# First head's query rows: SBUF-to-SBUF copies from the cast tiles instead of a read back from scratch

## The chip, the cores and the metric

One NeuronCore of one Trainium2 chip runs the whole program. The metric is the device time of one execution in microseconds. Three runs of the kernel before gave 1349.76, 1350.19 (the median) and 1351.14 us.

## The reference, cut to what matters

A gate mixes an attention branch and a SwiGLU branch over the same 2048 rows of x (512 wide). The attention has 32 query heads of 16 columns and one shared key and value head.

```
g = sigmoid((x * gate_w).sum(-1))
q = x @ wq            # 32 heads of 16
k = x @ wk;  v = x @ wv
a = softmax(q k^T / 4) v, heads joined, @ wo
b = (silu(x @ w_gate) * (x @ w_up)) @ w_down
out = g * a + (1 - g) * b
```

## The kernel before, in words

**Precision.** Products are made in float32r from a rounded part and a rest: `hi` and `lo`. A product of two such pairs is three matmuls. A head's query therefore occupies several groups of 16 rows: the rounded part, the rest, the rounded part again, and a row group of absolute values scaled by `kmax` (a bound on the keys, used in place of a row maximum). That makes 64 rows for a head, and two such sets of 64 rows (one for each pair of 512-column chunks) fill the 128 partitions of the tile `qs` (L667 multiplies `qs` with the keys `ks`).

**Making the queries.** `query(m, c)` makes the product for eight heads (m = 0 to 3) and one chunk of 512 rows of x (c = 0 to 3): 12 matmuls into a PSUM bank `pf`, of which there are three. When the last one is done, `keep` casts the bank into SBUF tiles `hh` (rounded), `hl` (rest) and a third one with the absolute values. For m = 0 the third one comes from the same buffers as `hh` and `hl`; each of these two names has seven buffers. In these tiles the partition is 8 times the row of a head plus the head, so one head's 16 rows stand 8 partitions apart. `store` then issues four DMAs of 256 KB on SyncE's queue, which write the tiles into the scratch tensor `q_d` in DRAM, sorted by head. When all chunks are there, one DMA of 512 KB reads a head's 128 rows back into `qs`: for head 0 at L643, for later heads in `load_head` (L653).

**The order at the start.** In a stage whose order is written out by hand, x is transposed, keys and values are made, then the four products of m = 0 run (called m0c0 to m0c3 here), then head 0 is loaded, and `fill(GAP)` runs three more products, m1c0 to m1c2, whole. After them the attention begins. A block of it takes two units (a unit is one head and 128 keys): scores into `pss` (two buffers, two matmuls of 64 rows each per half unit), exponentials on ScalarE (L675), and `mix`, which multiplies with the values (L687, 16 matmuls per block). The remaining products run between the scores as half matmuls of 64 rows ("low" and "high" half of the contraction). The first block has only low halves beside its scores, since a product's high half starts a fixed number of steps behind its low half. A one-element memset of `sign` on VectorE (L417) marks the end of a low half; the high half waits for it.

**What sets the order.** Each engine runs its own instructions in program order. The DMAs of SyncE's queue are issued in program order too, and an issue that waits holds up those behind it. The loads of the feed-forward weights stand outside the stage written by hand, so a scheduler places them.

Of the kernel before, what the change touches and what calls it, by code (L numbers as in the profile page):

```python
# [8 lines left out]
F32 = mybir.dt.float32  # L9
# [13 lines left out]
DH = 16  # L23
# [4 lines left out]
NCH = S // CH  # L28
TC = CH // P
NF = F // P  # L30
HG = P // DH
KR = 3 * DH
RT = 64
# [29 lines left out]
def tile_gated_mix(ctx, tc, x, wq, wk, wv, wo, w_gate, w_up, w_down, gate_w, out):  # L63
    nc = tc.nc
# [9 lines left out]
    q_d = dpool.tile([H, P, 2, CH], F32, name="q_d")  # L74
# [36 lines left out]
    def three(a, b, sa, sb):  # L111
        return [(a[0][sa], b[0][sb]), (a[0][sa], b[1][sb]), (a[1][sa], b[0][sb])]

    def mm(ps, terms):
        n = len(terms)
        for i, (a, b) in enumerate(terms):
            nc.tensor.matmul(ps, a, b, start=(i == 0), stop=(i == n - 1))  # L117
# [7 lines left out]
    def run(queue, n):  # L125
        for _ in range(min(n, len(queue))):
            queue.pop(0)()
# [7 lines left out]
    def load_split(view, name, bufs, pool=wp, order=lambda w, heads=True: w):  # L135
        shape = list(view.shape)
        raw = wp.tile(shape, F32, name="wraw", bufs=WRB)
        nc.sync.dma_start(raw, view)
        hi = pool.tile(shape, F32R, name=name + "h", bufs=bufs)
        lo = pool.tile(shape, F32R, name=name + "l", bufs=bufs)  # L140
        split(order(hi, False), order(lo, False), order(raw), nc.gpsimd, nc.gpsimd)
        return hi, lo
# [63 lines left out]
            for f in self.after:  # L206
                f()

    WQ, QS = {}, {}

    def by_row(w, heads=True):
        if heads:
# [3 lines left out]
    def load_wq(m):  # L216
        WQ[m] = load_split(wq_v[:, :, m * P:(m + 1) * P], f"wq{m}", 1, qpool, by_row)

    def query(m, c):
        cs = slice(c * CH, (c + 1) * CH)  # L220
        t = m * NCH + c

        def terms():
            r = []
            for k in range(KD):
                r += three(WQ[m], XC[c], (slice(None), k), (slice(None), k))
            return r

        def keep(ps):
            qh = wp.tile([P, CH], F32R, name="hh", bufs=7)  # L230
            ql = wp.tile([P, CH], F32R, name="hl", bufs=7)

            if m:
                qb = wp.tile([P, CH], F32, name="ht" if c % 2 else "hs", bufs=2)
                nc.vector.tensor_copy(qh, ps)
            else:
                qb = wp.tile([P, CH], F32R, name="hl" if c % 2 else "hh", bufs=7).bitcast(F32)
                nc.scalar.activation(qh, ps, AF.Copy)
                nc.scalar.activation(qb.bitcast(F32R), ps, AF.Abs, scale=kmax)
            nc.vector.tensor_tensor(ql, ps, qh.bitcast(F32), ALU.subtract)  # L240
            if m:
                nc.vector.tensor_scalar(qb, qh.bitcast(F32), kmax, None, op0=ALU.mult)
                nc.vector.scalar_tensor_tensor(qb.bitcast(F32R), qb, -1.0, qb, op0=ALU.mult, op1=ALU.max)
            parts = [ql, qh, qb.bitcast(F32R)]
            def store():
                for i, j in enumerate((1, 0, 1, 2)):
                    row = c % 2 * RT + i * DH
                    nc.sync.dma_start(q_d[m * HG:(m + 1) * HG, row:row + DH, c // 2, :].rearrange("h r s -> r h s"),
                                      parts[j].bitcast(F32))

            store()
            nc.vector.tensor_reduce(top[:, t:t + 1], qb, axis=AX.X, op=ALU.max)

        return Job(3 * KD, lambda: m in WQ, terms, keep)

    def queries():
# [238 lines left out]
    def new_qs(h):  # L495
        QS[h] = qsp.tile([P, 2, CH], F32R, name="qs")
        return QS[h]

    with tc.tile_pool(name="apool", bufs=1) as ap, tc.tile_pool(name="apool2", bufs=2) as a2:
        XT = {}  # L500

        def load_x(c, n):
            XT[c] = a2.tile([P, TC, D], F32, name="xt", bufs=2)
            for i in range(0, TC, n):
                t = c * TC + i
                nc.sync.dma_start(XT[c][:, i:i + n, :], x[t * P:(t + n) * P, :].rearrange("(i p) d -> p i d", p=P))
# [12 lines left out]
        def prepare_kv():  # L519
            k, v, g = slice(0, DH), slice(DH, 2 * DH), slice(2 * DH, 2 * DH + 1)  # L520
            for r in (0, RT):
                to = [w[:, :, r:r + 3 * DH].rearrange("p k (i n) -> p k i n", i=3) for w in (wkv_h, wkv_l)]
                src = wkv_f[:, :, k].unsqueeze(2).to_broadcast([P, KD, 3, DH])
                split(to[0], to[1], src, nc.vector)
            for to, src in ((3 * DH, v), (KW - 1, g)):
                rows = slice(to, to + src.stop - src.start)
                split(wkv_h[:, :, rows], wkv_l[:, :, rows], wkv_f[:, :, src], nc.vector)
# [12 lines left out]
        def zeros(n):  # L540
            for i in range(n):
                nc.tensor.matmul(pw[:, :P], warm, warm, start=True, stop=True)

        def transpose_x(c, i):
            if i == 0:
                if c < 2:
                    new_x(c)
                else:
                    new_x(c, qpool, str(c))
            xt, (xh, xl) = XT[c], XC[c]  # L550
            pt = ps_s.tile([P, 2 * CH], F32, name="pss")
            ptv = pt.rearrange("p (k t) -> p k t", k=KD)
            for j in range(2):
                for k in range(KD):
                    nc.tensor.transpose(ptv[:, k, j * P:(j + 1) * P], xt[:, i + j, k * P:(k + 1) * P], ident)
                if c == 0:
                    zeros(KEEP)
            hi = xh[:, :, i * P:(i + 2) * P]
            nc.scalar.activation(hi, ptv, AF.Copy)
            nc.vector.tensor_tensor(xl[:, :, i * P:(i + 2) * P], ptv, hi.bitcast(F32), ALU.subtract)  # L560
# [5 lines left out]
        def project_kv(c):  # L566
            cs = slice(c * CH, (c + 1) * CH)
            if c % 2 == 0:
                VZ[c // 2] = ap.tile([KW, 2 * CH], F32, name="vz", bufs=2)
            pk = ps_f.tile([P, CH], F32, name="pf")  # L570

            terms = [(w[:, k], XC[c][0][:, k]) for k in range(KD) for w in (wkv_h, wkv_l)]
            mm(pk[:KW, :], terms + [(wkv_h[:, k], XC[c][1][:, k]) for k in range(KD)])
            vz = VZ[c // 2][:, c % 2 * CH:(c % 2 + 1) * CH]
            nc.scalar.activation(vz, pk[:KW, :], AF.Copy)
            ka = a2.tile([DH, CH], F32, name="ka")
            nc.scalar.activation(ka, pk[:DH, :], AF.Abs)
            nc.vector.tensor_reduce(nk[:, c:c + 1], ka, axis=AX.X, op=ALU.max)

            for r in (0, RT):  # L580
                nc.gpsimd.tensor_copy(ks[r:r + 3 * DH, cs], vz[r:r + 3 * DH, :])
                lo = slice(r + 2 * DH, r + 3 * DH)
                nc.gpsimd.tensor_tensor(ks[lo, cs], vz[lo, :], ks[lo, cs].bitcast(F32), ALU.subtract)
# [19 lines left out]
        with tc.manual_schedule():  # L603

            warm = ap.tile([P, P], BF16, name="warm")
            nc.vector.memset(warm, 0.0)
            pw = ps_o.tile([P, CH], F32, name="po")
            zeros(WARM)
            load_wq(0)
            transpose_x(0, 0)  # L610
            prepare_kv()
            transpose_x(0, 2)
            prepare_norms()
            load_x(2, 2)
            transpose_x(1, 0)
            transpose_x(1, 2)
            load_x(3, 2)
            project_kv(0)
            transpose_x(2, 0)
            transpose_x(2, 2)  # L620
            project_kv(1)
            transpose_x(3, 0)
            transpose_x(3, 2)
            project_kv(2)
            store_x(2)
            transpose_v(0)
            project_kv(3)
            store_x(3)
            load_wq(1)
            load_wq(2)  # L630
            for c in range(NCH):
                job = query(0, c)
                for i in range(job.size):
                    if c == 0 and i == job.size - 1:
                        spread_k()
                    job.step(i)
                if c == 0:
                    transpose_v(1)

                    nc.vector.tensor_scalar(g_sb, g_sb, 0.5, 0.5, op0=ALU.mult, op1=ALU.add)  # L640
                    nc.vector.tensor_scalar(c_sb, g_sb, -0.5, 0.5, op0=ALU.mult, op1=ALU.add)
            load_wq(3)
            nc.sync.dma_start(new_qs(0).bitcast(F32), q_d[0])  # L643
            fill(GAP)


# [2 lines left out]
    with tc.tile_pool(name="bpool", bufs=2) as bp:  # L649
# [128 lines left out]
        with tc.manual_schedule():  # L778
# [25 lines left out]
            for k in range(2 * BEGIN // BLOCK, NB):  # L804
# [8 lines left out]
                h = u // NT  # L813
# [49 lines left out]
    with tc.If(rv != 0):  # L863
        with tc.tile_pool(name="gpool", bufs=2) as gp:
            with tc.For_i(0, H, 1) as h:
# [4 lines left out]
                for qt in range(NT):  # L870
# [3 lines left out]
                    for half in range(2):  # L874
                        ps = ps_s.tile([P, 2 * CH], F32, name="pss")
                        for j in range(2):
                            c = half * 2 + j
# [60 lines left out]
```

## Time and profile before

| what | value |
|---|---|
| median of three runs | 1350.19 us |
| the profiled execution's own time | 1349.22 us |
| its span (first to last instruction) | 1347.4 us |
| TensorE busy | 1330.7 us, 99% |
| ScalarE busy | 1069.5 us, 79% |
| VectorE busy | 710.9 us, 53% |
| GpSimd busy | 223.7 us, 17% |
| mean granted TensorE clock | 0.994 of full |

The profile counts the time of each engine's instructions inside one execution. "PE" is TensorE's matmul stream, "PEld" its weight loads, "DVE" VectorE, "ACT" ScalarE, "POOL" GpSimd, "SPq" the issuing of DMAs by SyncE. A list of waits names who stood idle and whose result ended the idle time. A table by windows gives each engine's busy time in a stretch, the granted clock (1.00 is full speed) and the share of time in which the DMA engines were busy. Spans of one line are start, duration and instruction, in microseconds from the span's start.

### The profile page before, as it was taken

What the parts mean: (1) busy time and instruction counts of PE and PEld (TensorE: products, weight loads), DVE (VectorE), ACT (ScalarE), POOL (GpSimd) and SP (SyncE); (2) the same over time, 40 slices, a digit from 0 to 9 for tenths busy, and PEclk for the clock granted to TensorE, in tenths of its full rate; (3) what the DMA queues carried; (4) which work ended last, traced back from release to release, by engine and by line L of the source; (5) the groups of instructions that cost most, each with busy time, mean ns of one, the idle gap of its engine ahead of it and who ended that gap; (6) DMA issues with size and microseconds to landing.
All of it is one profiled execution on the core that took longest, in us unless ns stands there. A gap on an engine that the chain in (4) does not pass through costs nothing. (4 is left out here: it accounts for less than half of the span.)

```text
span 1347.4 us, 26625 instructions
## 1 busy us (share of the span) xinstructions
PE 1330.7 (99%) x10743; PEld 763.8 (57%) x10743; DVE 710.9 (53%) x1219; ACT 1069.5 (79%) x1475; POOL 223.7 (17%) x227
## 2 busy tenths in 40 slices
PE   9899999999999999999999999999999999999998
PEld 7555555555555555555555555555555555555586
DVE  4546455555456555555455555455455555455442
ACT  4277888888888888888888888888888888888611
POOL 6340222043042052133020000000000000001223
PEclk9799999999999999999999999999999999999999
DMA  8855211122125173256053252242132342233154
GB/s 281 275 173 153 87 52 44 37 69 81 36 73 199 63 246 111 67 170 196 23 174 128 83 177 83 67 128 91 46 114 63 118 150 75 98 101 121 49 186 143
DMA packets 101040, 156.02 MB, mean 116 GB/s; under 512 B 11568, under 2 KB 42544, under 8 KB 99248
## 3 DMA queue, kind: packets, MB, share of 16 engines
q1 hardware_dynamic: 99184, 154.05, 35.7%
q8 instruction: 88, 1.44, 0.4%
q10 hardware_dynamic: 1728, 0.20, 0.1%
q14 instruction: 40, 0.33, 0.1%
HBM read 98.63 MB, written 55.57 MB: 114 GB/s over the span
## 5 line engine op out<-in xcount | busy, mean ns | idle before, releaser
L675 ACT ACTIVATE pt<-pss 128x1024 f32<-128x1024 f32 (+1 forms) x1024 | 842.4, 876 | 186.0 <-PE pss L667 146.4
L687 PE MATMUL po<-pt,vaug 128*32 128x512 f32 x4096 | 468.9, 597 | 0.0
L671 DVE COPY pt<-pss 128x512 f32<-128x512 f32 x354 | 244.9, 692 | 419.8 <-PE pss L667 386.9
L667 PE MATMUL pss<-qs,ks 64*128 64x512 f32 x2048 | 398.5, 417 | 7.1 <-DMA qs<-q_d 5.8
L667 PEld LDWEIGHTS pss<-qs,ks 64*128 64x128 f32 x2048 | 190.2, 184 | 227.3 <-ACT pt L675 183.9
L687 PEld LDWEIGHTS po<-pt,vaug 128*32 128x32 f32 x4096 | 119.3, 110 | 261.1 <-issue 255.9
L675 ACT ACTIVATE pt<-pt 128x512 f32<-128x512 f32 x354 | 195.6, 620 | 0.0
L192 PE MATMUL pf<-xh,wgl 64*128 64x512 f32 (+1 forms) x440 | 161.9, 392 | 0.0
L192 PE MATMUL pf<-xh,wgh 64*128 64x512 f32 (+1 forms) x440 | 160.3, 392 | 0.3
L192 PE MATMUL pf<-xl,wgh 64*128 64x512 f32 (+1 forms) x440 | 159.9, 390 | 0.0
L192 PE MATMUL pf<-xh,wuh 64*128 64x512 f32 (+1 forms) x440 | 158.0, 391 | 0.6 <-DVE sign L417 0.3
L192 PE MATMUL pf<-xl,wuh 64*128 64x512 f32 (+1 forms) x440 | 158.1, 390 | 0.0
L192 PE MATMUL pf<-xh,wul 64*128 64x512 f32 (+1 forms) x440 | 156.9, 391 | 0.0
L192 PE MATMUL pf<-wdh,hl 64*128 64x512 f32 (+1 forms) x427 | 143.3, 390 | 0.0
L192 PE MATMUL pf<-wdh,hh 64*128 64x512 f32 (+1 forms) x427 | 142.7, 391 | 0.0
L192 PE MATMUL pf<-wdl,hh 64*128 64x512 f32 (+1 forms) x427 | 142.7, 390 | 0.0
L696 DVE RECIPROCAL rsb<-rsb 128x128 f32<-128x128 f32 x128 | 117.1, 935 | 10.9 <-issue 8.6
L445 POOL CAST xh<-wraw 128x512 fp32r<-128x512 f32 x4 | 2.9, 726 | 535.6 <-DMA wraw<-o_d 535.6
L192 PEld LDWEIGHTS pf<-xh,wgh 64*128 64x128 f32 (+1 forms) x440 | 78.3, 185 | 10.1 <-issue 1.4
L192 PEld LDWEIGHTS pf<-xh,wuh 64*128 64x128 f32 (+1 forms) x440 | 77.1, 185 | 9.9 <-issue 1.6
L192 PEld LDWEIGHTS pf<-xl,wgh 64*128 64x128 f32 (+1 forms) x440 | 78.4, 185 | 5.9
L192 PEld LDWEIGHTS pf<-xh,wgl 64*128 64x128 f32 (+1 forms) x440 | 78.4, 185 | 5.7
(155 smaller groups left out, 1368.6 us busy)
## 6 DMA issues: line engine op xcount, KB each, us to landing
qs<-q_d SPq DMA_DIRECT2D x32, 512.0 KB, 4.7
q_d<-hh SPq DMA_DIRECT2D x34, 256.0 KB, 3.1
wraw<-in_B_w_gate_dram SPq DMA_DIRECT2D x28, 256.0 KB, 4.0
wraw<-in_B_w_up_dram SPq DMA_DIRECT2D x28, 256.0 KB, 3.2
wraw<-in_B_w_down_dram SPq DMA_DIRECT2D x28, 256.0 KB, 3.0
wgh<-w_d SPq DMA_DIRECT2D x28, 256.0 KB, 2.7
wgl<-w_d SPq DMA_DIRECT2D x28, 256.0 KB, 3.0
wuh<-w_d SPq DMA_DIRECT2D x28, 256.0 KB, 2.7
```

The costliest lines, as they stand in the source:

```text
L192: ins = nc.tensor.matmul(self.ps, a, b, start=(i == 0 and not half), stop=(last and half != 0))
L445: nc.gpsimd.tensor_copy(OT[c][0][:, k, :], raw)
L667: nc.tensor.matmul(ps[:, b * CH:(b + 1) * CH], ks[rows, kt * P:(kt + 1) * P], QS[h][rows, j, :], start=True, stop=True)
L671: other = nc.vector.tensor_copy(pt[:, CH:], ps[:, CH:]) if half else None
L675: ins = nc.scalar.activation(pt[:, w], ps[:, w], AF.Exp, scale=SCALE)
L687: nc.tensor.matmul(po[c * 2 * DH:(c + 1) * 2 * DH, :], vaug[:, kt, :], pt[:, c * CH:(c + 1) * CH], start=(kt == 0), stop=(kt == NT - 1))
L696: nc.vector.reciprocal(rsb[:, w], rsb[:, w])
```

## The change

For m = 0, `keep` now issues four small DMAs before anything else: each copies the 16 rows of head 0 out of a cast tile straight into its place in `qs` (16 partitions of 512 floats, 32 KB). The four stores of the chunk to `q_d` are not issued there any more; they are put in a list. After the last product of m = 0 the list is run: all 16 stores follow each other. The tile `qs` is allocated earlier, and the read of head 0 from `q_d` is gone. Products of m = 1 to 3 store as before, and the later heads are still read from `q_d`.

```
-    WQ, QS = {}, {}
+    WQ, QS, STORES = {}, {}, []
...
             parts = [ql, qh, qb.bitcast(F32R)]
+            if not m:
+                for h, qs in QS.items():
+                    for i, j in enumerate((1, 0, 1, 2)):
+                        row = c % 2 * RT + i * DH
+                        nc.sync.dma_start(qs[row:row + DH, c // 2, :].bitcast(F32),
+                                          parts[j].bitcast(F32).rearrange("(r h) s -> h r s", h=HG)[h])
+
             def store():
...
-            store()
+            if m:
+                store()
+            else:
+                STORES.append(store)
             nc.vector.tensor_reduce(top[:, t:t + 1], qb, axis=AX.X, op=ALU.max)
...
             load_x(3, 2)
+            new_qs(0)
             project_kv(0)
...
+            run(STORES, NCH)
             load_wq(3)
-            nc.sync.dma_start(new_qs(0).bitcast(F32), q_d[0])
             fill(GAP)
```

On SyncE's queue, before, the last stores of m0c3 are followed by two weight loads, the read of head 0 and the first stores of m1c0:

```order
L248 DMA q_d<-hl 16x8x512
L248 DMA q_d<-hh 16x8x512
L248 DMA q_d<-hl 16x8x512
L138 DMA wraw<-in_A_wq_dram 128x4x128
L138 DMA wraw<-in_B_w_gate_dram 128x4x128
L643 DMA qs<-q_d 128x1024
L248 DMA q_d<-hh 16x8x512
```

On the same queue, now, the copies into `qs` stand where the first stores of m = 0 stood; this is the seam between the last copies (L249, chunk m0c3) and the first stores (L255, chunk m0c0):

```order
L249 DMA qs<-hh 16x512 x3
L249 DMA qs<-hl 16x512
L249 DMA qs<-hh 16x512
L249 DMA qs<-hl 16x512
L255 DMA q_d<-hh 16x8x512
L255 DMA q_d<-hl 16x8x512
L255 DMA q_d<-hh 16x8x512 x3
L255 DMA q_d<-hl 16x8x512
```

All 16 copies stand ahead of all 16 stores; the load of the last query weights, the stores of m = 1, the read of head 1 and the feed-forward weights stand behind these stores. The end of that stretch, now, with the last stores of m1c2 and the read of head 1 (L664), is:

```order
L255 DMA q_d<-hl 16x8x512
L255 DMA q_d<-hh 16x8x512
L255 DMA q_d<-hs 16x8x512
L664 DMA qs<-q_d 128x1024
L138 DMA wraw<-in_B_w_gate_dram 128x4x128
L138 DMA wraw<-in_B_w_up_dram 128x4x128
```

Both feed-forward weight loads now stand behind the read of head 1, where one stood ahead of it.

On VectorE one instruction moves. Before, the casts of m1c2 and the marks of the low halves stand like this:

```order
L235 CAST hh_602<-pf_589 128x512
L240 TENSOR_TENSOR hl_603<-pf_589,hh_602 128x512
L242 TENSOR_SCALAR hs_604<-hh_602,kmax_84 128x512
L243 SCALAR_TENSOR_TENSOR hs_604<-hs_604 128x512
L252 TENSOR_REDUCE top_86<-hs_604 128x1
L417 MEMSET sign_85 1x1 x2
```

The same place now:

```order
L235 CAST hh_617<-pf_604 128x512
L427 MEMSET sign_85 1x1
L240 TENSOR_TENSOR hl_618<-pf_604,hh_617 128x512
L242 TENSOR_SCALAR hs_619<-hh_617,kmax_84 128x512
L243 SCALAR_TENSOR_TENSOR hs_619<-hs_619 128x512
L262 TENSOR_REDUCE top_86<-hs_619 128x1
L427 MEMSET sign_85 1x1
```

The mark of m1c3's low half moved up into the casts of m1c2, so that the subtraction behind it waits for that low half. The instructions of TensorE, ScalarE and GpSimd keep their order.

## The prediction

> **What bounds the kernel now.** First the totals and the clock line of the page, to see which engine sets the time and where it does not run at full speed.
>
> ```profile
> span 1347.4 us, 26625 instructions
> ...
> PE 1330.7 (99%) x10743; PEld 763.8 (57%) x10743; DVE 710.9 (53%) x1219; ACT 1069.5 (79%) x1475; POOL 223.7 (17%) x227
> ...
> PEclk9799999999999999999999999999999999999999
> ```
>
> TensorE is busy 99% of the span, so a microsecond is won only where TensorE idles or runs slowly. The second of 40 slices, 34 to 67 us, has a digit 7: it ran below its clock there. Next the list of TensorE's waits, its two longest rows (total, times, longest):
>
> ```profile
> PE pss L667 <- DMA qs<-q_d: 5.8, 1, 5.8
> PE pss L667 <- ACT pt L675: 1.1, 2, 0.9
> ```
>
> The one wait worth having is for the read of head 0 that the change removes. Now its place, in the timelines of TensorE and of SyncE's queue (start, duration; SyncE's duration is that of the issue):
>
> ```profile
> 47.58 0.39 PE L192 MATMUL pf<-xh,wq1l 128*128 128x512 f32 x1
> 53.77 1.22 PE L667 MATMUL pss<-qs,ks 64*128 64x512 f32 x4 [5.80 <-DMA qs<-q_d]
> ...
> 44.62 0.64 SPq L248 DMA_DIRECT2D q_d<-hl  x1
> 48.56 0.34 SPq L643 DMA_DIRECT2D qs<-q_d  x1
> ```
>
> TensorE finishes m1c2 at 47.97 (47.58 + 0.39) and stands until 53.77. The read can be issued only when the last store, issued at 44.62, has landed. So the chain there is store, landing, read, landing, first score. The windows around it give the clock (columns: busy time and count of each engine, then granted clock, DMA share, GB/s):
>
> ```profile
> 51.00:52.00 1.00, 0.00 (x0) 0.00 (x0) 0.97 (x2) 0.00 (x0) 1.00 (x1) 1.00 0.92 340
> 52.00:53.00 1.00, 0.00 (x0) 0.00 (x0) 0.97 (x1) 0.00 (x0) 1.00 (x2) 0.70 1.04 387
> 53.00:54.00 1.00, 0.23 (x2) 0.26 (x4) 0.69 (x1) 0.00 (x0) 0.92 (x2) 0.50 1.04 377
> ...
> 65.00:66.00 1.00, 1.00 (x11) 0.20 (x4) 0.00 (x0) 0.00 (x0) 0.60 (x1) 0.50 0.22 62
> 66.00:67.00 1.00, 1.00 (x12) 0.40 (x6) 0.00 (x0) 0.00 (x0) 0.92 (x2) 0.97 0.00 0
> ...
> 66.56:71.43 4.87, 4.87 (x44) 2.59 (x41) 0.06 (x1) 3.79 (x4) 3.63 (x5) 1.00 0.36 106
> ```
>
> The clock is halved at 52.4 (0.70 is 0.4 us at full and 0.6 at half), 4.4 us after TensorE fell idle, and it is back at 66.0. So the wait costs twice: 5.80 us of idleness, and about 12.3 us of work at half speed.
>
> **The change, part by part.** *The idle time.* What the first score needs now is the last copy. The last tile that a copy waits for is m0c3's rest (`hl`), and the queue is in order: that copy is the second of the chunk's four. First its cast, then the nearest row for the copy.
>
> ```profile
> 41.06 0.69 DVE L240 TENSOR_TENSOR hl<-pf,hh 128x512 fp32r<-128x512 f32 x1 [1.44 <-ACT hl L239]
> ...
> L701 SPq DMA_DIRECT2D o_d<-osb x4: 358/411/418, 126.9 to 128.2; - x4
> ...
> DMA to landing us min/median/max: 1.7/2.0/2.3
> ```
>
> Before shows no SBUF-to-SBUF copy. The nearest row is L701, which moves the same shape, 16 partitions of 512 floats, to DRAM: 0.41 us to issue and 2.0 us to landing. The rest is ready at 41.75; copies two to four issue at 41.75, 42.16 and 42.57, and the last lands near 44.6. TensorE arrives at 47.97: 3.4 us to spare. The other end is the price of a whole store, with its slowest rows:
>
> ```profile
> L248 SPq DMA_DIRECT2D q_d<-hh x16: 538/598/1259, 31.5 to 57.9; - x16
> ...
> DMA to landing us min/median/max: 2.8/3.9/5.4
> ```
>
> At 0.60 us per issue and 5.4 us to landing the last copy would be there at 41.75 + 1.2 + 5.4 = 48.4, 0.4 us late; at 1.26 per issue 49.7, 1.7 late. I take the L701 price, same shape and size: the idle term is **-5.80 us**, at worst -4.1. TensorE's own work covers the copies; without m1c0 to m1c2 ahead of the scores nothing would.
>
> *The slow clock.* TensorE's rows at half and at full speed, start to start:
>
> ```profile
> 54.76 0.62 PE L192 MATMUL pf<-xh,wq1h 64*128 64x512 f32 x1
> 55.19 0.62 PE L192 MATMUL pf<-xl,wq1h 64*128 64x512 f32 x1
> ...
> 66.56 0.73 PE L667 MATMUL pss<-qs,ks 64*128 64x512 f32 x4
> ...
> 71.43 0.73 PE L667 MATMUL pss<-qs,ks 64*128 64x512 f32 x4
> ...
> 1259.48 0.39 PE L192 MATMUL pf<-wdh,hl 64*128 64x512 f32 x1
> 1259.71 0.39 PE L192 MATMUL pf<-wdh,hh 64*128 64x512 f32 x1
> ```
>
> A lone half matmul takes 0.43 us at half and 0.23 at full speed. A block at full speed lasts 71.43 - 66.56 = 4.87 us: four score matmuls, six slots of products, a pair of scores, two slots, a pair, sixteen value matmuls. The first block has the same and eight more slots and two more pairs ahead of its value matmuls; a slot or a pair is 0.23. So it takes 4.87 + 10 x 0.23 = 7.17 us at full speed. In before it ran from 53.77 to 66.56, 12.79 us. The term is 7.17 - 12.79 = **-5.62 us**. ScalarE does not spoil it: it makes four exponentials in 3.79 us of each such block,
>
> ```profile
> 67.16 3.79 ACT L675 ACTIVATE pt<-pss 128x1024 f32<-128x1024 f32 x4 [2.59 <-PE pss L667]
> ```
>
> so six take 5.7 of the 7.17 us, and each score finds its buffer free (first exponential from 48.6, done at 49.6; third score wanted at 47.97 + 0.57 + 6 x 0.23 = 49.9). Ends of the term: nothing if the clock falls all the same, -6.4 (half of 12.79) if everything simply doubles its speed.
>
> *The moved stores.* The 16 stores start at about 43.0, behind the last copy's issue, instead of 31.5 to 45.3. Nobody reads m = 0's rows from scratch soon, but the tiles are held longer: `hh` has seven buffers, m = 0 takes six, m1c0 the seventh, and the cast of m1c1 needs m0c0's first one, read by that chunk's first and third store. It stood at 45.74:
>
> ```profile
> 45.74 0.68 DVE L235 CAST hh<-pf 128x512 fp32r<-128x512 f32 x1
> 46.46 0.69 DVE L240 TENSOR_TENSOR hl<-pf,hh 128x512 fp32r<-128x512 f32 x1
> ...
> 48.91 0.68 DVE L235 CAST hh<-pf 128x512 fp32r<-128x512 f32 x1
> ```
>
> The third store issues at 43.0 + 2 x 0.60 = 44.2 and lands 3.9 later, at 48.1: this **new wait** is 2.4 us. Queued behind it on VectorE are the rest of m1c1's casts, then m1c2's, then the mark of m1c3's low half. TensorE waits for them first when m2c0 needs the bank of m1c1, at 49.9 + 4 x 0.23 (pair, two slots, pair) + 4 x 0.23 (slots) = 51.7; the bank is free at 48.1 + 1.4 = 49.5. Cover 2.2 us, cost 0. At the slow end (1.26 per issue, 5.4 to landing) the store lands at 50.9, the bank is free at 52.3, and 0.6 us is lost. The subtraction that now waits behind the mark costs nothing: m1c2's cast follows m1c1's by 48.91 - 45.74 = 3.17 us, so it ends at 52.0, when m1c3's low half (twelve slots, done at 51.7) is over; its bank is wanted only by m2c1, a block later.
>
> *The queue behind.* Sixteen copies of 0.41 us come in, one read goes. While such stores run the DMA engines are full:
>
> ```profile
> 40.00:47.97 7.97, 7.97 (x36) 6.26 (x34) 6.51 (x11) 1.03 (x2) 0.00 (x0) 1.00 0.98 315
> ...
> 59.16 0.85 SPq L653 DMA_DIRECT2D qs<-q_d  x1
> ...
> 121.67 0.39 PE L192 MATMUL pf<-xh,wgh 64*128 64x512 f32 x1
> ```
>
> At 315 GB/s 256 KB takes 0.83 us: the sixteen end near 56, the weights and twelve stores of m = 1 near 67, and head 1's read goes out at 67 instead of 59, landing about 5 us later. Head 1 begins in the eighth block: 55.1 + 6 x 4.87 + 2 = 86 in the new time. Cover 14 us. The feed-forward weights are first used at 121.67, 110 then, and their loads go out from 68 on. Cost 0.
>
> *Sum.* -5.80 - 5.62 = -11.4 us. Every stage behind is TensorE's, so this reaches the end: 1349.22 - 11.4 = 1337.8 for an execution like the profiled one. That one lies 0.97 us under the median of the three; on the median, 1350.19 - 11.4 = **1338.8**.
>
> **The clock rule.** The row: TensorE was busy from 53.77, at half clock until 66.0, 12.3 us. The Trainium skill, "TensorE: Matmul & The Clock Gate", Part 1 (The HAM clock gate), says that about 3.4 us of sustained work release it and one idle window of about 3.4 us throttles it. By that rule the slow stretch would have been 3.4 us long and its removal worth 1.7, and the sum -7.5, 1342.7. The rows contradict the release and agree with the throttling (4.4 us after work stopped).
>
> **The rivals.** *The clock falls anyway.* It came back only 2.6 us after the value matmuls began:
>
> ```profile
> 63.42 3.20 PE L687 MATMUL po<-pt,vaug 128*32 128x512 f32 x16
> ```
>
> So lone half matmuls may not count as full activity, and the first block has 4.6 us of them. Then the idle term alone remains: 1350.19 - 5.8 = 1344.4; half of that stretch slow, 1341.6. Against it, near the end TensorE has only lone halves and score pairs for 4.8 us, from 1256.38 to the value matmuls at 1261.19, and the two windows there stay at 1.00:
>
> ```profile
> 1256.38 0.39 PE L192 MATMUL pf<-wdh,hh 64*128 64x512 f32 x1
> ...
> 1261.19 1.06 PE L687 MATMUL po<-pt,vaug 128*32 128x512 f32 x8
> ...
> 1255.00:1260.00 5.00, 4.98 (x33) 3.37 (x30) 2.33 (x5) 3.88 (x6) 0.00 (x0) 1.00 0.00 0
> 1260.00:1265.00 5.00, 5.00 (x42) 1.86 (x42) 1.95 (x3) 4.09 (x6) 0.00 (x0) 1.00 0.13 30
> ```
>
> *The copies are late*, at a store's price: 0.4 to 1.7 us of idleness, too short for the clock: 1339.2 to 1340.5. Partition strides of eight speak for it, the size against.
>
> *The stores block VectorE (slower).* If the sixteen stores share the DMA engines so that the third lands with the last, at 1.26 us each, that is 43.0 + 20.2 = 63.2. TensorE then waits for m1c1's bank from 51.7 to 64.6, 12.9 us, the clock falls too (5.6): -11.4 + 18.5 = +7.1, 1357.3. It turns slower than before once that landing passes about 56 (a wait of 5.8 and 5.6 for the clock). The landing row, 5.4 at most with seven stores around, speaks against it.
>
> *It does not do what it says*: were the first score still bound to the stores, it would start no earlier; 1350. The order shows the read gone, so little speaks for that.
>
> **How the numbers follow.** Forecast 0.75 (1337 to 1340); clock falls 0.09; copies late 0.07; stores block 0.04; no effect 0.03; a due date missed further on, anywhere between, 0.02. The range 1336.5 to 1342.0 takes in the first, the third and the milder half of the second, about 0.86; its low end is 1350.19 - 12.2 (clock term -6.4) less 1.5 for the spread of runs. Within 0.2%, 2.7 us, is what a measurement here cannot tell from no change. Faster: 0.75 + 0.09 + 0.07 + 0.01 = 0.92; same 0.03; slower 0.05.
>
> **What would show it.** The waits of TensorE have no row for `qs`, or one under 1 us; the clock line's second digit is 9; the first score starts at 48.0 and the next block's at 55; VectorE's cast of m1c1 starts near 48 and waits for a store; the copies land within 2.5 us. A clock of 0.50 anywhere in 50 to 66 us, or a TensorE wait on m1c1's bank, makes the prediction wrong.

## The result, and the profile after

Six runs of the changed kernel have a median of 1339.73 us (1339.41 to 1340.38), six of the kernel before 1350.66 us. The ratio is 0.9915, 95% interval 0.9901 to 0.9929: 10.9 us less, where 11.4 was forecast. The profiled execution took 1339.43 us, against 1349.22 before.

First the totals and the clock line of the page after:

```profile
span 1337.6 us, 26645 instructions
...
PE 1325.0 (99%) x10743; PEld 760.6 (57%) x10743; DVE 707.3 (53%) x1219; ACT 1068.4 (80%) x1475; POOL 223.2 (17%) x227
...
PEclk9999999999999999999999999999999999999999
```

The second digit of the clock line is 9 now, and TensorE's busy time fell by 5.7 us with the same number of matmuls: the matmuls that ran at half clock are the ones that got shorter. The list of TensorE's waits after (total, times, longest):

```profile
PE pss L678 <- ACT pt L686: 1.1, 2, 0.9
PE pss L565 <- DMA xt<-in_A_x_dram: 1.1, 1, 1.1
...
PE pf L192 <- POOL wuh L107: 0.5, 1, 0.5
...
PE pf L192 <- POOL wul L108: 0.4, 1, 0.4
```

The 5.8 us row is gone. Two rows are new, on GpSimd's split weights `wuh` and `wul`; they come back below. TensorE's timeline at the place (start, duration):

```profile
47.53 0.39 PE L192 MATMUL pf<-xh,wq1l 128*128 128x512 f32 x1
47.85 0.73 PE L678 MATMUL pss<-qs,ks 64*128 64x512 f32 x4
48.42 0.39 PE L192 MATMUL pf<-xh,wq1h 64*128 64x512 f32 x1
48.65 0.39 PE L192 MATMUL pf<-xl,wq1h 64*128 64x512 f32 x1
...
55.13 0.73 PE L678 MATMUL pss<-qs,ks 64*128 64x512 f32 x4
```

The scores follow the last whole product without a gap, lone halves start 0.23 us apart, and the second block starts at 55.13, where it stood at 66.56: 11.43 us earlier. SyncE's queue, VectorE's new wait, and the copies (issue time, then time to landing, each as least, median and most):

```profile
43.43 0.54 SPq L249 DMA_DIRECT2D qs<-hl  x1
44.02 0.59 SPq L255 DMA_DIRECT2D q_d<-hh  x1
...
66.73 0.84 SPq L664 DMA_DIRECT2D qs<-q_d  x1
67.66 0.64 SPq L138 DMA_DIRECT2D wraw<-in_B_w_gate_dram  x1
```

```profile
45.09 0.69 DVE L262 TENSOR_REDUCE top<-hs 128x1 f32<-128x512 f32 x1
48.53 0.69 DVE L235 CAST hh<-pf 128x512 fp32r<-128x512 f32 x1 [2.76 <-DMA q_d<-hh]
```

```profile
L249 SPq DMA_DIRECT2D qs<-hh x10: 533/560/613, 31.4 to 42.8; - x10
...
DMA to landing us min/median/max: 1.9/1.9/3.1
```

The last copy goes out at 43.43, and all are in `qs` before TensorE asks. VectorE waits 2.76 us for a deferred store, and TensorE does not notice.

### The profile page after: what moved, and what is told of

Same layout as the page of the kernel before. It is cut to its first block, busy times and chain, and to the rows that moved or that the text cites. A ratio compares the mean times of both kernels' runs of the same rounds, so it can differ in the third digit from the quotient of the medians.

```text
span 1337.6 us, 26645 instructions
## 1 busy us (share of the span) xinstructions
PE 1325.0 (99%) x10743; PEld 760.6 (57%) x10743; DVE 707.3 (53%) x1219; ACT 1068.4 (80%) x1475; POOL 223.2 (17%) x227
## 5 line engine op out<-in xcount | busy, mean ns | idle before, releaser
L192 PEld LDWEIGHTS pf<-xh,wgh 64*128 64x128 f32 (+1 forms) x440 | 78.3, 185 | 10.2 <-issue 1.6
```

The source lines that it names most:

```text
L192: ins = nc.tensor.matmul(self.ps, a, b, start=(i == 0 and not half), stop=(last and half != 0))
```

## The experiments

Each is the kernel before or the changed one with one edit. Times are medians beside runs of the kernel before on the same chip (1350.32 us for the first four, 1350.51 for the last three); a ratio is to that kernel, with its 95% interval.

### 1. The wait stays, TensorE is kept busy in it

To the kernel before:

```
             fill(GAP)
+            pw = ps_o.tile([P, CH], F32, name="po")
+            zeros(80)
```

> The kernel before, with 80 matmuls of zeros on TensorE (128x128, results not used) put into the wait for the read of head 0. They take about 5 us and end before the read lands at 53.8, so the first score cannot start earlier; only the clock can change. My theory: the slow clock is a term of its own, caused by the idle time: the clock stays at 1.00, the first block lasts 7.2 us instead of 12.8, the second block starts at 60.9 instead of 66.6, and the time is 5.6 us under before: about 1344.6 (up to 1345.6 if about 1 us is given back further on). Rival: the lone half matmuls of the first block are what brings the clock down, idle or not: the clock falls between 53 and 60 all the same and the time is 1350.

Measured: 1344.63 us, ratio 0.9956 (0.9940 to 0.9973). TensorE's timeline, then a window over the first block (the column ahead of the last two is the granted clock):

```profile
48.53 4.64 PE L542 MATMUL po<-warm 128*128 128x128 bf16 x80
53.70 0.73 PE L669 MATMUL pss<-qs,ks 64*128 64x512 f32 x4 [0.53 <-DMA qs<-q_d]
...
60.95 0.73 PE L669 MATMUL pss<-qs,ks 64*128 64x512 f32 x4
```

```profile
56.00:61.00 5.00, 5.00 (x35) 2.52 (x33) 0.06 (x1) 4.07 (x5) 0.00 (x0) 1.00 0.96 305
```

The first score starts where it did, at 53.70, and the second block 5.61 us earlier than before. So the clock is a term of its own, 5.6 us, and idleness causes it: with 80 useless matmuls in the wait it is gone, though lone halves run as before. The rival falls.

### 2. Copies without the deferral

To the changed kernel:

```
-            if m:
-                store()
-            else:
-                STORES.append(store)
+            store()
```

> The changed kernel, but with the four stores of a chunk right behind its four copies again (one half of the change undone). SyncE then issues 16 copies of 0.54 us and 12 stores of 0.6 us ahead of the end of m0c3's copies: 15.9 us from 31.4, so the last copy goes out near 47.3 and lands 1.9 to 4 us later, at 49.2 to 51.3; TensorE idles 1.3 to 3.4 us. My theory: the deferral is worth this idle time, but the clock holds, since the idle time is under the 4.4 us after which it fell before: 1341 to 1343. Rival one: the copies alone are the change, the stores' place does not matter: 1339.7. Rival two: among the stores a copy lands as late as a store (5.4 us) and the clock falls as well: 1348 or more.

Measured: 1347.60 us, ratio 0.9975 (0.9965 to 0.9986). TensorE, SyncE's queue and the windows:

```profile
52.94 0.47 PE L675 MATMUL pss<-qs,ks 64*128 64x512 f32 x1 [3.76 <-DMA qs<-hl]
```

```profile
50.43 0.54 SPq L249 DMA_DIRECT2D qs<-hl  x1
```

```profile
53.00:54.00 1.00, 1.00 (x6) 0.82 (x7) 0.00 (x0) 0.56 (x1) 0.00 (x0) 0.84 1.02 356
54.00:57.00 3.00, 3.00 (x10) 2.33 (x10) 0.00 (x0) 1.49 (x2) 0.00 (x0) 0.50 0.95 265
...
63.00:64.00 1.00, 1.00 (x12) 0.07 (x4) 0.00 (x0) 0.00 (x0) 0.00 (x0) 0.54 1.05 356
```

Of the 10.9 us, the copies alone bring 2.7. Twelve stores in the same queue push the last copy from 43.43 to 50.43, TensorE idles 3.76 us, and the clock falls at 53.7 and is back at 63.9. My theory was wrong on the clock: I had it hold under 4.4 us of idle time. The first rival, that the stores' place does not matter, is refuted; the second has the clock right, but not the landing, which takes 3.5 us at most in that kernel.

### 3. Whole products right behind the wait

To the kernel before:

```
             for j in range(2):
                 exps(*score(0, j))
+            fill(24)
             for n in range(BEGIN):
```

> The kernel before, with the same wait, but the next two products (24 matmuls over all 128 rows) run whole right behind the first scores, ahead of the lone halves. The clock is at half from 52.4 on as before. My theory: it stayed low until 66.0 because lone half matmuls do not count enough to release it; whole ones do, so it is back within two windows of 3.4 us of 53.8, between 57 and 61, and the execution takes 2 to 4 us less than before. Rival: once it has fallen it stays low for a fixed time of 13.6 us whatever TensorE does: back at 66.0, time as before.

Measured, in one execution: 1354.98 us. Its time says little on the clock: two products more are done at the start, so that fewer are left for the later blocks, and at the end TensorE has new waits on VectorE, ScalarE and GpSimd (1.8, 1.3 and 1.2 us). The clock is what it was made for:

```profile
56.16 0.79 PE L192 MATMUL pf<-xh,wq1h 128*128 128x512 f32 x1
```

```profile
52.00:53.00 1.00, 0.00 (x0) 0.00 (x0) 0.96 (x2) 0.00 (x0) 1.00 (x1) 0.84 0.83 299
...
59.00:60.00 1.00, 1.00 (x5) 0.82 (x4) 0.00 (x0) 0.00 (x0) 0.00 (x0) 0.75 0.89 285
60.00:61.00 1.00, 1.00 (x6) 0.81 (x5) 0.24 (x1) 0.00 (x0) 0.00 (x0) 1.00 0.83 277
```

It falls at 52.7 and is back at 59.5, 3.3 us after the first whole product. A fixed time of 13.6 us is refuted: what TensorE does sets the return, and lone halves are slow to bring it about. The expected gain of 2 to 4 us did not come; that part of the expectation failed.

### 4. Less work ahead of the scores

To the changed kernel:

```
-            fill(GAP)
+            fill(GAP - 24)
...
             for j in range(2):
                 exps(*score(0, j))
+            fill(24)
```

> The changed kernel with two of the three whole products taken from ahead of the first scores and put right behind them; the work is the same. TensorE wants the scores at 42.5 instead of 47.9, the last copy, issued at 43.4, lands near 45.4. My theory: TensorE waits 2.9 us, too short for the clock, and this shows both where the copies land and what the cover was worth: 1342.6. Rival one: the clock falls already after such a wait: another 5 us, 1347 or more. Rival two: the earlier start of ScalarE pays the wait back: 1339.7 or less.

Measured: 1343.91 us, ratio 0.9946 (0.9925 to 0.9967).

```profile
42.71 1.01 PE L678 MATMUL pss<-qs,ks 64*128 64x512 f32 x3
45.83 0.46 PE L678 MATMUL pss<-qs,ks 64*128 64x512 f32 x1 [2.10 <-DMA qs<-hl]
```

```profile
46.00:47.00 1.00, 1.00 (x3) 0.69 (x3) 0.08 (x1) 0.67 (x1) 0.00 (x0) 0.62 0.94 301
47.00:49.00 2.00, 2.00 (x7) 1.51 (x6) 0.00 (x0) 0.35 (x1) 0.00 (x0) 0.50 0.92 306
49.00:50.00 1.00, 1.00 (x5) 0.82 (x4) 0.00 (x0) 0.00 (x0) 0.00 (x0) 0.67 0.98 252
```

The copies are in `qs` at 45.8, so in the changed kernel they have 2 us to spare. The first three matmuls run ahead of the last copies, so only 2.10 us are idle, and even that brings the clock down, for 3.4 us (46.24 to 49.66). It is cheap here: whole products follow, and one stretch of 3.4 us is all that runs slowly. My theory's total was near, but the clock fell, so rival one is right on the mechanism and wrong on its size. ScalarE's earlier start pays nothing back.

### 5. A third buffer for raw weights

To the changed kernel:

```
-WRB = 2
+WRB = 3
...
-            ka = a2.tile([DH, CH], F32, name="ka")
+            ka = a2.tile([DH, CH], F32, name="ka", bufs=1)
```

> The changed kernel with three instead of two buffers for the raw weights that GpSimd splits (one buffer less for a small tile of the first stage makes the room). The changed kernel is 11.43 us ahead of before at the second block, but 10.5 at the end: 0.95 us goes at 598 us, where two products wait for GpSimd's split of the up weights, and 0.25 near the end. My theory: the chain raw load, split, next raw load has under 1 us of room there, and a small shift of a load uses it up; with a third raw buffer the loads go out earlier, those two waits go, and the lead stays near 11.4: about 1338.7. Rival: the loss is in the DMA landing itself and the third buffer moves nothing: 1339.7, with the waits still there.

Measured: 1339.63 us (1338.57 to 1340.91), ratio 0.9922 (0.9908 to 0.9936): no different from the changed kernel. TensorE's two longest waits and the last two:

```profile
PE pss L565 <- DVE xl L570: 1.6, 1, 1.6
PE pss L678 <- ACT pt L686: 1.1, 2, 0.9
...
PE pf L192 <- DVE sign L427: 0.3, 2, 0.2
PE pss L678 <- DVE sign L427: 0.2, 1, 0.2
```

The waits on `wuh` and `wul` are gone, but that they hang on the buffer is not shown. This execution was late by 1.6 us at its first scores (49.48), with a slow clock at 11.6 to 15.0 us in the transposing stage, and TensorE reached the place of the two waits at 595.68, 1.88 us later than in the changed kernel (593.80). The load of the up weights did not go out earlier than there: 594.65 against 594.21, both times right behind the store of a split weight on SyncE's queue. So the waits can be gone because TensorE came later. The times do not show the gain, and whether the 0.95 us can be had stays open.

### 6. The deferred stores land later

To the changed kernel:

```
+            store_x(2)
             run(STORES, NCH)
```

> The changed kernel with the two stores of x's third chunk (2 MB) issued a second time between the last copy and the first of the deferred stores, with the same data, so that the deferred stores land later. By 315 GB/s that is 6.7 us: the third store lands at 55 instead of 48.5, the bank of m1c1 is free at 56.4, TensorE needs it at 51.7 and waits 4.7 us; the clock falls as well (it fell after 2.1 us and after 3.8 us of idle time in the runs so far) and stays low through the lone halves. My theory: this is the place where the deferral has its price, 4.7 plus 3 to 6 us: 1347 to 1351. Rival: VectorE's late casts never reach TensorE, the bank is not what it waits for: 1339.7.

Measured: 1344.78 us, ratio 0.9957 (0.9942 to 0.9972). VectorE, then TensorE, then the windows:

```profile
54.06 0.69 DVE L235 CAST hh<-pf 128x512 fp32r<-128x512 f32 x1 [1.36 <-DMA q_d<-hh]
```

```profile
55.62 0.47 PE L192 MATMUL pf<-xh,wq2h 64*128 64x512 f32 x1 [3.04 <-DVE hl L240]
...
57.96 2.72 PE L699 MATMUL po<-pt,vaug 128*32 128x512 f32 x16
```

```profile
56.00:57.00 1.00, 1.00 (x7) 0.75 (x5) 0.97 (x2) 0.20 (x1) 0.00 (x0) 0.60 1.03 303
...
59.00:60.00 1.00, 1.00 (x12) 0.13 (x6) 0.93 (x3) 0.10 (x1) 0.00 (x0) 0.69 1.00 332
```

The deferral's price stands where the prediction put it: m2c0's first matmul waits for m1c1's bank, whose cast waits for a deferred store. Its size is smaller than I wrote. The store landed at 54.0, not 55, so the wait is 3.04 us and not 4.7; and the clock was low only from 56.2 to 59.6, a stretch in which the block's value matmuls began (57.96). One thing the edit moved besides: in this kernel the mark of m1c3's low half stands ahead of m1c1's casts on VectorE. It was done at 52.70, and the store, which came after it, set the start of the cast; the last 1.36 us are the store's alone.

### 7. Stores on another queue

To the changed kernel:

```
-            if m:
-                store()
-            else:
-                STORES.append(store)
+            store()
...
-                    nc.sync.dma_start(q_d[m * HG:(m + 1) * HG,
+                    (nc.sync if m else nc.scalar).dma_start(q_d[m * HG:(m + 1) * HG,
...
```

> The changed kernel, but the stores of m = 0 are not deferred; they go out on ScalarE's DMA queue, right behind each chunk's casts, while SyncE's queue holds only the copies. Three of the last four stores stand behind the first exponential in ScalarE's order and push the second one back by up to 1.8 us. My theory: what the deferral does is to keep the stores from standing ahead of the copies in one queue; with two queues the copies go out as early as in the changed kernel and land 2 to 3.5 us later, before 47.9, and no tile is held long: 1339.7 to 1341.5. Rival: the stores delay the copies in the DMA engines, whatever the queue: the copies land after 50, the clock falls, 1345 or more.

Measured: 1341.47 us, ratio 0.9936 (0.9921 to 0.9951). TensorE's wait and what stands behind it, the last copy's issue, and the copies' times to landing:

```profile
47.67 0.46 PE L675 MATMUL pss<-qs,ks 64*128 64x512 f32 x1 [1.09 <-DMA qs<-hh]
48.06 0.50 PE L192 MATMUL pf<-xh,wq1h 128*128 128x512 f32 x1
...
51.01 0.49 PE L675 MATMUL pss<-qs,ks 64*128 64x512 f32 x1
```

```profile
47.92 0.54 SPq L249 DMA_DIRECT2D qs<-hl  x1
```

```profile
DMA to landing us min/median/max: 2.2/2.7/3.5
```

The time is in the expected range, but not by the expected way. The last copy goes out at 47.92, not at 43.43 as in the changed kernel: ScalarE makes the cast of m0c3 at 44.77 instead of 39.80, since its casts now stand behind the stores that it issues. That copy lands at 50.1 at the earliest (2.2 us), after 47.9. TensorE does not stand still for it, because its order is another in this kernel: m1c2, which the changed kernel runs ahead of the scores, stands between the third and the fourth score here, 12 whole matmuls from 48.06 to 51.01. So 1.09 us is not what late copies would cost in the changed kernel's order, and the 6.1 us that come back against experiment 2 can't be put down to the second queue alone. The clock holds through those 1.09 us. The rival has the last copy's landing right, but by its late issue and not by the DMA engines, and the clock and the time wrong.

What the deferral buys is told by the copies' own rows instead. With stores in flight on another queue they take 2.7 us to land instead of 1.9, and with stores in their own queue (experiment 2) 2.4; but there the last copy goes out 7.0 us later, 0.6 of it because the first one did. In one queue the copies are late mostly by the issues that stand ahead of them, and much less by sharing the DMA engines.

## Why the prediction was right, point by point

- **The idle time** (-5.80): right. The wait is gone, and experiment 4 puts the copies at 45.8. The issue price was too low, 0.56 us where 0.41 was taken, so the last copy went out at 43.43 instead of 42.57; the landing, 1.9 us at the median, was as taken. One copy took 3.1 us, over the 2.5 that the prediction named as a sign; the 3.4 us that the sum had to spare covered both.
- **The slow clock** (-5.62): right. Experiment 1 alone gives 5.61 us. Both terms together are 11.43 us at the second block, where 11.42 was worked out.
- **The moved stores** (cost 0): right. The cast of m1c1 stands at 48.53 (48.1 forecast) behind a wait of 2.76 us (2.4). Its bank was free at 49.95 and m2c0 began at 51.79, so the cover was 1.8 us (2.2). Experiment 6, where the store landed 5.5 us later, shows that the wait then reaches TensorE where it was placed.
- **The queue behind** (cost 0): right for the loads that it names. Head 1's read goes out at 66.73 (67 forecast), the weights at 67.66 (68).
- **The sum reaches the end**: not fully, and this is the one step that failed. "Every stage behind is TensorE's" left out that some stages have almost no room. The load of an up weight and GpSimd's split of it, in the timelines of the two kernels:

```profile
604.61 0.38 SPq L138 DMA_DIRECT2D wraw<-in_B_w_up_dram  x1
```

```profile
607.87 0.61 POOL L107 CAST wuh<-wraw 128x512 fp32r<-128x512 f32 x1 [1.31 <-PE pss L667]
```

```profile
594.21 0.39 SPq L138 DMA_DIRECT2D wraw<-in_B_w_up_dram  x1
```

```profile
597.43 0.61 POOL L107 CAST wuh<-wraw 128x512 fp32r<-128x512 f32 x1 [1.74 <-PE pss L678]
```

  11.43 us earlier the split would start at 596.44, so it is 1.0 us late, and TensorE waits 0.5 and 0.4 us for its two results. The rows name TensorE as what ended GpSimd's wait, but the load tells more: it is 1.0 us late too (594.21 for 593.18), and it lands 3.1 us behind its issue in both kernels, 0.1 to 0.2 us ahead of the split. So it is the load that came late; why it did not move by the whole 11.43 us stays open. TensorE's lead is 11.41 us ahead of this place (593.80 against 605.21) and 10.45 behind it (600.49 against 610.94). Then the last matmul, before and after:

```profile
1341.54 0.39 PE L117 MATMUL pf<-wo3h,xl 128*128 128x512 f32 x1
```

```profile
1331.06 0.39 PE L117 MATMUL pf<-wo3h,xl 128*128 128x512 f32 x1
```

  So 10.48 of 11.43 us arrive at the last matmul of this execution. The span shrank by 9.8, since what follows that matmul took 0.7 us longer in this execution; over the runs the medians differ by 10.9.
- **The rivals.** *The clock falls anyway*: no; with no wait in front, the first block's lone halves left it at 1.00. *Copies late*: no, 2 us to spare; that up to 1.7 us of idleness would be too short for the clock was not safe to say, since 2.1 us brought it down in experiment 4. *Stores block VectorE*: real as a mechanism, 1.8 us away. *A due date missed further on*: this one took its 0.95 us.
- **The clock rule**: the slow stretch was worth 5.6 us, not the 1.7 of the rule on release. The agreement with the rule on throttling did not last: experiments 2, 4 and 6 show the fall after 3.8, 2.1 and 3.0 us of idle time.

## What to carry to other kernels

A wait on the engine that sets the time can cost twice: price the time behind it by the granted clock, row by row, before judging what removing it is worth. When small urgent transfers and large patient ones share a queue, their order can be worth more than the transfers themselves: here 2.7 us for the copies and 8 more for moving the stores behind them. What is moved back holds its buffers longer; find which instruction needs the first of them, and keep that distance.

## What the runs showed of the hardware that was not expected

| kernel | idle before | clock low | for | what ran meanwhile |
|---|---|---|---|---|
| experiment 7 | 1.09 us | never | | whole products to 51.0, then lone halves |
| experiment 4 | 2.10 us | 46.2 to 49.7 | 3.4 us | whole products |
| experiment 6 | 3.04 us | 56.2 to 59.6 | 3.4 us | lone halves, value matmuls from 57.96 |
| experiment 2 | 3.76 us | 53.7 to 63.9 | 10.2 us | lone halves, value matmuls from 61.2 |
| before | 5.80 us | 52.4 to 66.0 | 13.6 us | lone halves, value matmuls from 63.4 |
| experiment 3 | 6.53 us | 52.7 to 59.5 | 6.8 us | idle to 55.0, whole products from 56.2 |

Each low stretch is one, two, three or four times 3.4 us. The Trainium skill, "TensorE: Matmul & The Clock Gate", Part 1 (The HAM clock gate), gives a free-running window of that length, and the table agrees with it. The runs differ in two points from what that part says. One idle window is said to throttle: here 2.1 us of idle time was enough, and the fall can come after work has resumed (53.7 in experiment 2, where TensorE had restarted at 52.94). The length of one wait does not decide alone: in the transposing stage, waits of 1.7 and 1.6 us left the clock at 1.00 in experiments 1 and 7, and one of 1.6 us was followed by a fall at 11.6 in experiment 5; what made the difference is not shown. And a busy window is said to release: windows filled with half matmuls of 64 rows and score pairs did not, in before and in experiment 2, while 3.4 us with whole products, or with value matmuls in part of it, did. That the gate weighs the rows in use fits all six, but no run here separates rows from other differences of these instructions. The same lone halves did not bring a full clock down: 4.9 us of them ran through the first block of the changed kernel at 1.00.

The start before 48 us also varies: the first scores started at 47.85 in the changed kernel, at 48.47 in experiment 6, where TensorE has the same instructions up to there, and at 49.48 in experiment 5, which has one small buffer less in that stretch. A gain under 1 us can't be read from the end time of one execution.
